# Three loads at the head of the kernel begun by ScalarE's queue in place of SyncE's

## The chip, the cores and the metric

The kernel runs on one core of one Trainium2 chip. The metric is device time in microseconds (us); the time of the kernel before is 755.41 us, the median of 3 runs (755.40 to 755.68). Engines are named as in the profile: PE (TensorE matmul), PEld (its weight loads), DVE (VectorE), ACT (ScalarE), POOL (GpSimd), SP (SyncE). SPq is the instruction queue of SP, from which transfers are begun.

## The reference

An attention with 32 memory slots per head, then two feed-forward layers, in float32:

```
a   = softmax(phi, over the 576 positions)          # (4, 8, 576, 32)
k_m = a^T k ; v_m = a^T v                           # per batch and head: 32 x 64
x   = softmax(q k_m^T / sqrt(64)) v_m               # (4, 8, 576, 64) -> 2304 x 512
h   = x w_in ; g = max(0.01 h, h) ; y = g w_out     # w_in 512x2048, w_out 2048x512
out = ((y w_a) * (y w_b)) w_out2                    # 512x1536, 512x1536, 1536x512
```

## The kernel before

The kernel is one long list of small operations (`op(...)`), each with one engine, what it reads and what it writes. A table written out by hand, ORDER, gives the order in which all of them are emitted, and so the order within each engine's instruction queue; a second table, PLACES, gives each tile its room in SBUF or PSUM (s0 to s36 are rooms of 4 KB per partition). Nothing is reordered afterwards: an engine takes its instructions in the order of the table. Semaphores stand between engines and between a transfer and its users.

Attention goes by batch b (0 to 3) and by group g of four heads (0 and 1). For one (b, g), `kv_part` loads phi and two tiles of k and v (`kv`, 512 KB each, and a rest `kvr`), takes the exponential of phi (L454, ACT, its maximum from DVE at L448), transposes it on PE (`t_a` L503, `t_z` L507/L509) and copies it to SBUF (`en`, L311 on ACT), multiplies it with k and v on PE (`km`, L525), divides by the sum (L541, ACT, `kvn`), transposes the result (`kvt`, L551) and copies it out (`kd` and `vm`, L311). `q_load` brings q; `sc_both` makes the scores (`sc`, L620) and their softmax on DVE and ACT. `vw_unit` multiplies v's part with w_in (L690), `h_unit` makes h (L735).

A weight is loaded by `weight`, in 64-bit words (`raw`, 512 KB, L393), and put into another format by three ACT instructions and two of DVE: high (L403), sign (L410), low (L407), clamp (L414), join (L418). The first two weight tiles of w_in are here called win(0,0) and win(0,1).

Transposes named `warm` fill PE's time at the head; they are counted out in the same table.

All input loads are begun on SP's queue, in the table's order: phi(0,0), phi(0,1), phi(1), win(0,0), kvr, kv(0,1,0), kv(0,1,1), kv(0,0,0), kv(0,0,1), two tiles of q, then win(0,1), win(0,2), win(0,3), two more of q, and so on. Here kv(b, g, i) is the i-th tile of a pair.

What the table has in ACT's order at the head, with the loads of the change at the words where they stand among ACT's instructions:

```
word  6  load phi(0,1)
word  8  exponential of phi(0,0)      word 13  exponential of phi(0,1)
word 20  copy en of group 0           word 24  copy en of group 1
word 26  exponential of phi(1), g=1   word 28  copy en (L516) of t_z of group 0
word 31  load win(0,0)
word 32  high of win(0,0)  (L403)     word 35  copy en (L516) of t_z of group 1
word 37  exponential of phi(1), g=0
word 39  load kv(0,1,0)
word 40  sign of win(0,0)  (L410)
```

PE's order around them: t_z of group 0 (L509), t_z of group 1, transposes of phi(1), km of group 1 from `kvr` (it needs the copy of word 35), four `warm`, a t_z of phi(1), km of group 1 from kv(0,1,0) and kv(0,1,1), km of group 0 in three parts with kvt of group 1 among them, the scores of group 1, kvt of group 0, the scores of group 0.

Rooms: kv(0,1,0) and win(0,1) have the same one (s1), so the load of win(0,1) waits until km of group 1 has read kv(0,1,0). Win(0,2) has the room of win(0,0) (s13) and waits for its low. Win(0,3) has a fresh room and stands behind both on SP's queue.

Of the kernel before, what the change touches and what calls it, by code (L numbers as in the profile page):

```python
# [16 lines left out]
B, H, S, D, M = 4, 8, 576, 64, 32  # L17
DM, DFF, DFF2 = 512, 2048, 1536
P = 128
# [52 lines left out]
def c_dve(n):  # L72
    return 0.16 + n * 1.03e-3
# [6 lines left out]
def c_dma(nbytes):  # L80
    return max(0.6, nbytes / DMA_RATE)
# [195 lines left out]
def tile_mem_attention__leaky_mlp__bilinear_mlp(  # L277
# [13 lines left out]
    nc = tc.nc  # L291
# [8 lines left out]
    op, tile_of = pr.op, pr.tile  # L300
# [80 lines left out]
    def weight(kind, c, k=0, after=(), split=True, late=False):  # L381
        key, raw, low_t = (kind, c, k), ("raw", kind, c, k), ("lw", kind, c, k)
        cv, half = cv_of(kind, c, k)
        tile_of(raw, "slot", [512], I64)
        if cv not in pr.specs:
            tile_of(cv, "slot", [2, 512], I32)
        tile_of(low_t, "t", [512], I32)
        if split:
            tile_of(key, "slot", [2, 512], F32R)

        def load(T):
            src = src_of[kind](c, k)
            nc.sync.dma_start(T[raw] if len(src.shape) == 2 else T[raw].rearrange("p (j f) -> p j f", j=src.shape[1]), src)  # L393

        def words(T, t, w):
            return T[raw].bitcast(t).rearrange("p (n t) -> p n t", t=2)[:, :, w]

        def part(T, t, w):
            return T[low_t].bitcast(t).rearrange("p (n t) -> p n t", t=2)[:, :, w]


        def high(T):
            nc.scalar.activation(T[cv][:, half, :].bitcast(F32), words(T, F32, 1), AF.Abs, scale=2.0 ** 16)  # L403


        def low(T):
            nc.scalar.activation(part(T, U16, 0), words(T, U32, 0), AF.Copy, scale=0.937 * 2.0 ** -29)  # L407

        def sign(T):
            nc.scalar.activation(part(T, F16, 1), words(T, F32, 1), AF.Copy, scale=2.0 ** -120)  # L410

        def clamp(T):
            x = T[cv][:, half, :].bitcast(F32)
            nc.vector.tensor_scalar(x, x, W_LEAST, W_MOST, op0=ALU.max, op1=ALU.min)  # L414

        def join(T):
            x = T[cv][:, half, :]
            nc.vector.scalar_tensor_tensor(x, x, 3, T[low_t], op0=ALU.logical_shift_left, op1=ALU.bitwise_or)  # L418

        a, lt = ("a", key), ("l", key)  # L420
        op("DMA", c_dma(524288), load, r=after, w=[raw], tiles=[raw], ahead=1e12 if late else 45.0)
        op("ACT", 0.66, high, r=[raw], w=[a], tiles=[raw, cv, low_t])
        op("ACT", 0.66, low, r=[raw], w=[lt], tiles=[raw, low_t, cv])
        op("ACT", 0.8, sign, r=[raw], w=[("s", key)], tiles=[raw, low_t, cv])
        op("DVE", 0.42, clamp, w=[a], tiles=[cv])
        op("DVE", 0.68, join, r=[lt, ("s", key)], w=[a], tiles=[cv, low_t])
        if kind == "win" and c == 0 and k > 1:
            idle(cv, lambda t: t[:, half, 0:P].bitcast(F32), a)
        if not split:
            return  # L430
        op(copy_by(512), 0, lambda T, e: copy(e, T[key][:, 0, :], fp(T, kind, c, k)), r=[a], w=[("hi", key)], tiles=[cv, key])
        op("DVE", c_dve(512), lambda T: minus(T[key][:, 1, :], fp(T, kind, c, k), T[key][:, 0, :].bitcast(F32)), r=[a, ("hi", key)], w=[key], tiles=[cv, key])
# [31 lines left out]
    def kv_part(b, g):  # L464

        phi, en, kvn = ("phi", b, g) if b == 0 else ("phi", b), ("en", b, g), ("kvn", b, g)
        kvt = [("kv", b, g, 0), ("kv", b, g, 1)]
        rest = ("kvr", b // 2)

        lot = slice(b % 2 * 64, b % 2 * 64 + 64)  # L470
        if b == 0:
            tile_of(phi, "slot", [1, S])
            op("DMA", c_dma(P * S * 4), lambda T: nc.sync.dma_start(T[phi], phiT[b, :, g:g + 1, :]), w=[("e", b, g)], tiles=[phi])
        elif g == 0:
            tile_of(phi, "big", [2, S])
            op("DMA", c_dma(P * S * 8), lambda T: nc.sync.dma_start(T[phi], phiT[b]), w=[("e", b, 0), ("e", b, 1)], tiles=[phi], keep=2)

        def ph(T):
            return T[phi][:, g if b else 0, :]

        ek = ("e", b, g)
        tile_of(en, "slot", [5, P])
        tile_of(kvn, "t", [2, 2, D])
        for i, k in enumerate(kvt):
            tile_of(k, "slot", [2, 512])
            op("DMA", c_dma(P * 4096), lambda T, i=i, k=k: nc.sync.dma_start(T[k], kv[b, g, :, 2 * i:2 * i + 2, :]), w=[k], tiles=[k], keep=6 if b else 0)
        if g == 0 and b % 2 == 0:
            tile_of(rest, "slot", [2, 512])
            op("DMA", c_dma(P * 4096), lambda T: nc.sync.dma_start(T[rest], kv_rest[b:b + 2].rearrange("b p g f -> (b p) g f")), w=[rest], tiles=[rest], keep=6 if b else 0)

        st = [stat((n, b % 2), 2) for n in ("nmx", "es", "er")]
        er, ker = st[2][:, g:g + 1], ("er", b % 2, g)
        if b == 0:
            phi_stats(b, [g], phi, st)
        elif g == 0:
            phi_stats(b, [0, 1], phi, st)
        ta, tz = ("ta", b, g), ("tz", b, g)
        tile_of(ta, "x", [4, P])
        tile_of(tz, "x", [P])

        def t_a(T):
            for t in range(4):
                nc.tensor.transpose(T[ta][:, t, :], ph(T)[:, t * P:(t + 1) * P], ident)  # L503

        def t_z(T):
            if b % 2:
                nc.tensor.transpose(T[tz], ph(T)[:, S - P:S], ident)  # L507
            else:
                nc.tensor.transpose(T[tz][0:64], ph(T)[:, 4 * P:S], ident)  # L509

        op("PE", 0.45, t_a, r=[ek], w=[ta], tiles=[phi, ta])
        op("PE", 0.12, t_z, r=[ek], w=[tz], tiles=[phi, tz])
        op(copy_by(512), 0, lambda T, e: copy(e, T[en][:, 0:4, :], T[ta]), r=[ta], w=[(en, 0)], tiles=[ta, en])
        if b == 0:
            idle(en, lambda t: t[:, 0, :], (en, 0))
        op(copy_by(128), 0, lambda T, e: copy(e, T[en][lot, 4, :], T[tz][lot]), r=[tz], w=[(en, 1)], tiles=[tz, en])  # L516
        km = ("km", b, g)
        tile_of(km, "x", [P])

        def k_m(T, ts, first, last):  # L520
            for t in ts:
                n = slice(P) if t < 4 else lot
                src = T[kvt[t // 2]][:, t % 2, :] if t < 4 else T[rest][lot, g, :]
                for h in range(4):
                    nc.tensor.matmul(  # L525
                        T[km][h * M:(h + 1) * M, :], T[en][n, t, h * M:(h + 1) * M], src[:, h * P:(h + 1) * P],
                        start=first and t == ts[0], stop=last and t == ts[-1], skip_group_check=True,
                    )

        parts = KM_FIRST[g] if b == 0 else ((0, 1, 2, 3, 4),)  # L530
        for i, ts in enumerate(parts):
            need = list(dict.fromkeys(kvt[t // 2] if t < 4 else rest for t in ts))
            op(
                "PE", 0.29 * len(ts) + 0.05, lambda T, i=i, ts=ts: k_m(T, ts, i == 0, i == len(parts) - 1),
                r=[(en, 0), *([(en, 1)] if 4 in ts else []), *need], w=[km], tiles=[en, *need, km],
            )

        def norm(T, e):
            src = T[km].rearrange("p (c d) -> p c d", c=2).unsqueeze(2).to_broadcast([P, 2, 2, D])
            if e == "ACT":  # L540
                nc.scalar.activation(T[kvn], src, AF.Copy, scale=er)  # L541
            else:
                nc.vector.tensor_scalar_mul(T[kvn], src, er)

        op({"DVE": c_dve(256), "ACT": c_act(256)}, 0, norm, r=[km, ker], w=[kvn], tiles=[km, kvn])
        o = ("kvt", b, g)
        tile_of(o, "x", [2, P])

        def k_t(T):
            for i in range(2):  # L550
                nc.tensor.transpose(T[o][:, i, :], T[kvn][:, i].rearrange("p c d -> p (c d)"), ident)  # L551

        op("PE", 0.25, k_t, r=[kvn], w=[o], tiles=[kvn, o])

        op(copy_by(128), 0, lambda T, e: copy(e, kd[b % 2][:, g, :], T[o][:, 0, :]), r=[o], w=[("kd", b % 2, g)], tiles=[o])
        op(copy_by(128), 0, lambda T, e: copy(e, vm[:, b, g, :], T[o][:, 1, :]), r=[o], w=[("vm", b, g)], tiles=[o])
# [802 lines left out]
    for c, b in UNITS:  # L1359
        p, l = divmod(b, 2)  # L1360
# [20 lines left out]
        else:  # L1381
            if not whole(c, b):
                for j in range(2):
                    g = g_of(c, b, j)
# [85 lines left out]
```

## Time and profile before

| what | value |
|---|---|
| median of 3 runs | 755.41 us |
| the profiled execution | 756.11 us, of which the span is 754.3 us |
| PE busy | 746.6 us (99% of the span) |
| DVE, ACT busy | 688.8 us, 493.3 us |
| chain that ended last | PE 97%, ACT 1%, DMA 1% |
| DMA | 145.75 MB; nearly all engines busy in the first three of 40 slices |

The span is divided in 40 slices on the page; the first is 18.9 us long and holds all that the change touches. An idle time in brackets behind a row is that of the engine just before the instruction, and the arrow names what ended it.

### The profile page before, as it was taken

Reading aid. Unit: us, or ns where it says so; the run is one execution under the profiler, and the core shown is the slowest. Engines: PE = TensorE matmul, PEld = TensorE weight load, DVE = VectorE, ACT = ScalarE, POOL = GpSimd, SP = SyncE. Lnnn points to the kernel's source line nnn. Section 1 sums busy time; section 2 is a strip of 40 time slices with the busy share of each in tenths; the row PEclk is TensorE's granted clock in tenths of the full one; section 3 lists DMA queues with packets and bytes.
Section 4 is the critical chain, followed back from the end, with each engine's and each line's share of the span. In section 5 each row is a group of like instructions: output and inputs, shape, how many; then the busy total and the mean of one; then the engine's idle time right before and its main releaser. Section 6 shows DMA issues by size and latency. Waiting matters only on the chain.

```text
span 754.3 us, 12116 instructions
## 1 busy us (share of the span) xinstructions
PE 746.6 (99%) x4492; PEld 618.5 (82%) x4492; DVE 688.8 (91%) x1115; ACT 493.3 (65%) x962; POOL 3.4 (0%) x9
## 2 busy tenths in 40 slices
PE   8999999999999999999999999999999999999997
PEld 7656788887888789888888888888888888888885
DVE  2899988999999899999988989999999999789897
ACT  5898988796778786965767468487474424534430
POOL 0000000000000000000000000000000000000000
PEclk9999999999999999999999999999999999999999
DMA  9994233531342124167964466588896576584423
GB/s 324 388 407 168 83 113 126 163 117 57 112 139 82 47 84 140 56 209 244 346 219 168 141 207 237 195 280 292 262 382 243 208 259 233 177 309 167 158 72 113
DMA packets 56698, 145.75 MB, mean 193 GB/s; under 512 B 6976, under 2 KB 20544, under 8 KB 56640
## 3 DMA queue, kind: packets, MB, share of 16 engines
q1 hardware_dynamic: 56208, 143.41, 54.0%
q0 software_dynamic: 432, 1.57, 1.1%
q8 instruction: 35, 0.57, 0.3%
q14 instruction: 23, 0.19, 0.1%
HBM read 101.97 MB, written 41.42 MB: 190 GB/s over the span
## 4 chain that ended last, share of the span: by engine, by line
PE 97%; ACT 1%; DMA 1%; DVE 0%; issue 0%; POOL 0%; SPq 0%; POOLq 0%
PE abx L1098 17%; PE h L750 13%; PE ys_x L890 10%; PE abz L1098 9%; PE os_x L1297 8%; PE ys_z L890 5%; PE aby L1098 4%; PE os_z L1297 4%; PE o L1201 4%; PE yl L834 3%; PE ys_y L890 3%; PE a L1143 2%; PE b L1143 2%; PE vw L690 2%; PE os_y L1297 2%; PE y L800 2%
## 5 line engine op out<-in xcount | busy, mean ns | idle before, releaser
L1098 PE MATMUL abx<-yb_T,wo 128*128 128x512 f32 x432 | 108.4, 390 | 0.0
L1098 PEld LDWEIGHTS abx<-yb_T,wo 128*128 128x128 f32 x432 | 80.3, 188 | 16.2
L750 PE MATMUL h<-ahi,vwh 128*128 128x320 f32 (+1 forms) x240 | 73.4, 306 | 0.0
L311 ACT COPY ok<-os_x 128x512 f32<-128x512 f32 x66 | 38.0, 587 | 50.6 <-PE os_x L1297 46.9
L750 PE MATMUL h<-ahi,vwl 128*128 128x320 f32 (+1 forms) x240 | 71.0, 296 | 0.0
L750 PE MATMUL h<-alo,vwh 128*128 128x320 f32 (+1 forms) x240 | 70.9, 296 | 0.0
L711 ACT ACTIVATE bt<-h 128x256 f32<-128x256 f32 x120 | 45.1, 389 | 23.3 <-PE h L750 22.3
L750 PEld LDWEIGHTS h<-ahi,vwh 128*128 128x128 f32 x240 | 45.3, 189 | 12.2 <-issue 3.7
L311 ACT COPY pf<-abx 128x512 f32<-128x512 f32 x48 | 27.8, 585 | 36.7 <-PE abx L1098 35.0
L750 PEld LDWEIGHTS h<-alo,vwh 128*128 128x128 f32 x240 | 45.4, 189 | 1.5
L750 PEld LDWEIGHTS h<-ahi,vwl 128*128 128x128 f32 x240 | 45.4, 189 | 0.0
L316 DVE TENSOR_TENSOR sl_T<-bt,sh_T 128x1024 fp32r<-128x1024 f32 x28 | 34.2, 1221 | 3.0 <-ACT sh_T L311 2.3
L1098 PE MATMUL aby<-yb_B,wo 128*128 128x512 f32 x144 | 36.7, 390 | 0.0
L1098 PE MATMUL abx<-yb_B,wo 128*128 128x512 f32 x144 | 36.7, 390 | 0.0
L1098 PE MATMUL abz<-yb_T,wo 128*128 128x512 f32 x144 | 36.4, 389 | 0.0
L1098 PE MATMUL abz<-yb_B,wo 128*128 128x512 f32 x144 | 36.1, 389 | 0.0
L1297 PE MATMUL os_x<-pb_T,w 128*128 128x512 f32 x132 | 35.2, 389 | 0.0
L316 DVE TENSOR_TENSOR bt<-bt,bt 128x1024 f32<-128x1024 f32 x28 | 34.0, 1220 | 0.8 <-ACT bt L711 0.5
L311 ACT CAST sh_T<-bt 128x1024 fp32r<-128x1024 f32 x26 | 27.3, 1051 | 7.2 <-DVE bt L316 6.9
L311 ACT COPY u<-abx 128x512 f32<-128x512 f32 x24 | 14.0, 586 | 27.6 <-PE abx L1098 26.2
L1098 PEld LDWEIGHTS abz<-yb_T,wo 128*128 128x128 f32 x144 | 27.0, 188 | 5.6
L1098 PEld LDWEIGHTS abz<-yb_B,wo 128*128 128x128 f32 x144 | 26.9, 188 | 5.5
(327 smaller groups left out, 2051.9 us busy)
## 6 DMA issues: line engine op xcount, KB each, us to landing
k_wo<-wo SPq DMA_DIRECT2D x32, 512.0 KB, 5.2
wo<-k_wo SPq DMA_DIRECT2D x32, 512.0 KB, 4.8
raw_wout<-in_w_out_dram SPq DMA_DIRECT2D x24, 512.0 KB, 4.2
raw_win<-in_w_in_dram SPq DMA_DIRECT2D x16, 512.0 KB, 5.5
kv<-in_kv_dram SPq DMA_DIRECT2D x16, 512.0 KB, 9.0
wf<-k_wf SPq DMA_DIRECT2D x11, 512.0 KB, 5.8
raw_wb<-in_w_b_dram SPq DMA_DIRECT2D x8, 512.0 KB, 5.7
raw_wa<-in_w_a_dram SPq DMA_DIRECT2D x8, 512.0 KB, 4.6
```

The costliest lines, as they stand in the source:

```text
L311: nc.scalar.copy(dst, src)
L316: nc.vector.tensor_tensor(dst, a, b, op=alu)
L690: nc.tensor.matmul(rows_of(T, os, b, g, j, i), vm[half, b, g, head], w, start=True, stop=True)
L711: nc.scalar.activation(dst, src, AF.Prelu, alpha=0.01)
L750: nc.tensor.matmul(T[o], T[w[u]][:, k, fs], T[a[v]][:, k, cols], start=k == 0 and y == 0, stop=k == 1 and y == 2)
L800: nc.tensor.matmul(T[o], fp(T, *ws[j])[:, at], T[g_of(c, b, j)][:, i, :], start=f == 0, stop=f == 3)
L834: nc.tensor.matmul(T[o], T[ws[j]][:, u, w_left(c, 2 * eh + j, i, x)], T[hl[v]][:, f, :], start=f == 0 and y == 0, stop=f == 3 and y == 2)
L890: nc.tensor.matmul(T[o], lhs(T, u, w_left(c, 0, kk, x)), T[hl[v]][:, kk, :], start=i in (1, 2, 5) and kk == 0 and y == 0, stop=kk == 1 and ...
L1098: nc.tensor.matmul(T[o], T[w][:, which, u, k * P:(k + 1) * P], T[ys[v]][:, k, :], start=first and k == 0 and x == 0, stop=k == 1 and x == ...
L1143: nc.tensor.matmul(T[o], T[w][:, k // 2, u, k % 2 * P:(k % 2 + 1) * P], T[ys[v]][:, k, :], start=(k == 0 and x == 0), stop=(k == 3 and x = ...
L1201: nc.tensor.matmul(T[o], T[w][:, u, es], right(T, x, v), start=(x == 0 and k == 0), stop=(x == 1 and k == 2))
L1297: nc.tensor.matmul(T[o], lhs(T, u), T[g][:, v, :], start=i in (1, 2, 5) and k == 0, stop=k == 2, skip_group_check=True)
```

## The change

Three of the loads are begun with `nc.scalar.dma_start`, so that the instruction that begins them stands in ACT's queue: phi(0,1), win(0,0) and kv(0,1,0). ORDER and PLACES are the same, so each stands on ACT's queue at the word it has in the table. All other loads stay on SP's queue.

```diff
@@ weight, load
-            nc.sync.dma_start(T[raw] if len(src.shape) == 2 else T[raw].rearrange("p (j f) -> p j f", j=src.shape[1]), src)
+
+            (nc.scalar if key == ("win", 0, 0) else nc.sync).dma_start(T[raw] if len(src.shape) == 2 else T[raw].rearrange("p (j f) -> p j f", j=src.shape[1]), src)
@@ kv_part
-            op("DMA", c_dma(P * S * 4), lambda T: nc.sync.dma_start(T[phi], phiT[b, :, g:g + 1, :]), w=[("e", b, g)], tiles=[phi])
+            op("DMA", c_dma(P * S * 4), lambda T: (nc.scalar if g else nc.sync).dma_start(T[phi], phiT[b, :, g:g + 1, :]), w=[("e", b, g)], tiles=[phi])
@@ kv_part
-            op("DMA", c_dma(P * 4096), lambda T, i=i, k=k: nc.sync.dma_start(T[k], kv[b, g, :, 2 * i:2 * i + 2, :]), w=[k], tiles=[k], keep=6 if b else 0)
+            op("DMA", c_dma(P * 4096), lambda T, i=i, k=k: (nc.scalar if (b, g, i) == (0, 1, 0) else nc.sync).dma_start(T[k], kv[b, g, :, 2 * i:2 * i + 2, :]), w=[k], tiles=[k], keep=6 if b else 0)
```

## Rows read from the trace of the kernel before

**Rows 1.** The page's chain that ended last, share of the span by engine.
```profile
PE 97%; ACT 1%; DMA 1%; DVE 0%; issue 0%; POOL 0%; SPq 0%; POOLq 0%
```
**Rows 2.** Busy time by stretch: PE, PEld, DVE, ACT, POOL, PEclk, DMA share, GB/s.
```profile
24.00:57.00 33.00, 32.47 (x352) 19.12 (x353) 29.59 (x59) 29.20 (x71) 0.00 (x0) 1.00 1.02 399
```
**Rows 3.** Order of time, SP's queue, the first 20 us: start, length, line, transfer.
```profile
0.74 0.87 SPq L473 DMA_DIRECT2D phi<-in_phiT_dram  x2
...
2.12 0.43 SPq L393 DMA_DIRECT2D raw_win<-in_w_in_dram  x1
...
3.11 2.93 SPq L486 DMA_DIRECT2D kv<-in_kv_dram  x4
6.08 1.62 SPq L568 DMA_DIRECT2D q<-in_qT_dram  x2
13.39 1.42 SPq L393 DMA_DIRECT2D raw_win<-in_w_in_dram  x3
```
**Rows 4.** Waits of SP's queue from 7.7 to 14 us: total, times, longest.
```profile
SPq L393 <- DMA kv<-in_kv_dram: 3.7, 1, 3.7
SPq L393 <- PE km L525: 1.9, 1, 1.9
```
**Rows 5.** Order of time, ACT, the first 20 us.
```profile
3.84 1.28 ACT L454 ACT_TABLE_LOAD   x1 [3.84 <-DMA phi<-in_phiT_dram]
...
10.16 0.25 ACT L311 COPY en<-tz 64x128 f32<-64x128 f32 x1
10.30 0.69 ACT L403 ACTIVATE cv_win<-raw_win 128x512 f32<-128x512 f32 x1
...
11.82 0.77 ACT L410 ACTIVATE lw_win<-raw_win 128x512 f16<-128x512 f32 x1
...
16.30 0.47 ACT L541 ACTIVATE kvn<-km,er 128x256 f32<-128x256 f32 x1
18.72 0.27 ACT L311 COPY kd<-kvt 128x128 f32<-128x128 f32 x1 [1.95 <-PE kvt L551]
...
19.66 0.68 ACT L403 ACTIVATE cv_win<-raw_win 128x512 f32<-128x512 f32 x1 [0.50 <-DMA raw_win<-in_w_in_dram]
```
**Rows 6.** Order of time, PE, 9 to 20 us.
```profile
9.14 0.27 PE L509 MATMUL tz<-ident,phi 128*64 128x128 f32 x1
...
11.64 0.42 PE L525 MATMUL km<-kvr,en 64*32 64x128 f32 x8
...
12.69 1.08 PE L525 MATMUL km<-kv,en 128*32 128x128 f32 x32
...
15.59 0.64 PE L525 MATMUL km<-kv,en 128*32 128x128 f32 x16
17.68 0.64 PE L620 MATMUL sc<-q,kd 64*32 64x256 f32 x8 [1.45 <-DMA q<-in_qT_dram]
18.25 0.44 PE L551 MATMUL kvt<-ident,kvn 128*128 128x128 f32 x2
```
**Rows 7.** Issues of 512 KB loads: the last figure is us to landing.
```profile
raw_wout<-in_w_out_dram SPq DMA_DIRECT2D x24, 512.0 KB, 4.2
...
raw_wa_-1_3787<-in_w_a_dram SPq DMA_DIRECT2D x1, 512.0 KB, 3.4
```
**Rows 8.** The loads of raw_win issued in the first 40 us.
```profile
DMA to landing us min/median/max: 6.2/7.1/10.4
```
**Rows 9.** Busy time by stretch, columns as in Rows 2: a short gap, and the end.
```profile
16.00:17.00 1.00, 0.23 (x10) 0.00 (x0) 0.23 (x2) 0.74 (x2) 0.00 (x0) 1.00 1.05 385
...
751.00:752.50 1.50, 0.11 (x2) 0.00 (x0) 0.36 (x1) 0.00 (x0) 0.00 (x0) 1.00 0.85 305
...
753.50:754.30 0.80, 0.00 (x0) 0.00 (x0) 0.00 (x0) 0.00 (x0) 0.00 (x0) 0.50 0.00 0
```
**Rows 10.** Pieces of the chain that ended last: start, length, what.
```profile
1.36 6.20 PE warm L343 x36
...
8.00 0.44 PE warm L343 x4
```

## The prediction

> **What bounds the kernel now.** I read the page's chain of waits first: 97% of it is PE [rows 1], so what counts is how late PE's steady work begins and whether anything holds it up afterwards. The busy time by stretch shows where it becomes steady: from 24 to 57 us PE is busy 32.47 of 33 us [rows 2], and from there to the end I found no stall that could take a delay back. In that stretch the DMA share is 1.02 as well, so the transfers have no room to catch up either. A delay D at about 24 us is therefore D at the end, and the question is D. For it I read the first 20 us in order of time, queue by queue: SP, ACT, PE [rows 3 to 6]. What the reader is to see there is that SP's queue begins win(0,0) at 2.12 and the four kv tiles from 3.11 on, long before anyone needs them, because SP has nothing else to do. ACT comes to the same words of the table much later: the copy in front of win(0,0) runs at 10.16 and the sign behind kv(0,1,0) at 11.82 [rows 5].
>
> **phi(0,1).** It is the first instruction of ACT's queue, so nothing holds it; it leaves at about 0.74 beside phi(0,0) in place of 0.43 later (two issues take 0.87 [rows 3]). Gain: at most that 0.43. Loss: phi(0,0) now shares the DMA engines and may land later by about the same, and it releases ACT's first work at 3.84. PE has its 36 counted `warm` to 7.56 [rows 10], which cover half a microsecond either way. I take 0, ends -0.4 and +0.4.
>
> **win(0,0).** The load now stands behind the copy of word 28. Does ACT's queue hold it there? The trace has no load begun by ACT; the nearest rows say yes. ACT's table load reads no data of this program and still began at 3.84, when phi had landed [rows 5]: it stood behind a wait. And on SP's queue the three loads of raw_win leave together at 13.39 [rows 3], although the third has a free room: it stood behind the first. So the load leaves when the copy's own wait is over, which is t_z's end on PE at 9.14 + 0.27 = 9.41 [rows 6], or at the latest when the engine has done the copy, 10.41 [rows 5]. I take 9.45: instructions start before the one ahead has ended (10.30 against 10.16 + 0.25 [rows 5]), so the queue is ahead of the arithmetic. To landing: 3.4 us is a quiet load of the same size, 4.2 the median of 24 [rows 7], and 6.2 the fastest raw_win of the head, where all loads stood in one row [rows 8]. ACT's load has a row of its own, but shares the engines with SP's kv tiles; I take 4.2, so T = 13.7, ends 12.8 and 16.6. Its high, with the rest of ACT's queue behind it, begins at 13.7, not 10.30. That alone would cost little; kv behind it is worse.
>
> **kv(0,1,0).** Ahead of it on ACT's queue stand the high, which waits for T, a copy and an exponential. It leaves between T (the queue ahead of the arithmetic) and T + 1.52 (from 10.30 to 11.82 [rows 5]); I take 14.0, near the first for the reason above. By then SP's first loads are nearly through, so the landing is the quiet one: 14.0 + 3.4 = 17.4, ends 16.2 (12.8 + 3.4) and 22.3 (16.6 + 1.52 + 4.2). Before, it had landed at 11.4: SP's two q loads end at 7.70 [rows 3], and SP then waited 3.7 us for it [rows 4]. PE's km of group 1 began at 12.69 [rows 6]; now it begins at 17.4, later by 4.7.
>
> **What that becomes.** From the start of this km to the end of the last km of group 0 PE needed 16.23 - 12.69 = 3.54 us [rows 6], then it waited 1.45 for q. That q lands no later now, since the same bytes are asked for and two loads have gone to the back. So the scores begin at 20.9, not 17.68, and the 1.45 is slack. Group 0 follows: kvn 0.07 after its km and 0.47 long, kvt 0.44, the copies [rows 5, 6]. After them ACT was idle for 0.50 until win(0,1) landed [rows 5]. SP may begin win(0,1) only when km has read kv(0,1,0), because they share a room (the 1.9 us wait [rows 4]); it left 0.70 after km's start and now leaves at 18.1, with a quiet queue ahead: 21.5 to 22.3 by 3.4 and 4.2. ACT is ready for it at 22.4, so the 0.50 is slack too. D1 = 4.7 - 1.45 - 0.50 = 2.75. The queue of the transfers stands nearly empty from about 17 to 20; everything behind win(0,1) on SP moves by about 2 to 3 us, no more than the engines do, so it adds nothing.
>
> **The clock.** PE's fillers are counted out, so the new waits leave it idle: from about 11.6, until ACT's copy releases the km from `kvr` [rows 6] at about 14.6, and again until 17.4, with about 1.3 us of work between. [...] Its price is in the first row of the chain: the 36 `warm` took 6.20 us from a cold start, at 0.11 each they would have taken 3.96 [rows 10], a loss of 2.24. Of the 4.6 us from km at 17.4 to kvt at 22.0, 0.54 is ACT, so 88% of it bears: D2 = 2.0, ends 0 and 2 x 2.24.
>
> **Sum.** The profiled execution is 756.11 us, 754.3 of it span; 756.11 + 2.75 + 2.0 = 760.9. It lies 0.70 above the median, so the median goes from 755.41 to 760.2.
>
> **Rivals.**
> *The clock holds* (0.22): gaps of 3 and 2 us with some work between are not the empty end of the kernel. Then D = 2.75: 758.2, own range 757.0 to 760.
>
> *ACT's queue runs ahead of waits* (0.20), the case in which it is not slower. The place is the hand-over to ACT: if an instruction that waits is set aside and the queue goes on, the loads leave while the earlier instructions still wait. It decides at two points: win(0,0) must leave by about 6.1 (10.30 - 4.2) and kv(0,1,0) by about 8.5 (12.69 - 4.2). Then nobody waits for either, the same bytes pass through full engines, and only the 0.43 of the first issue is left: 755.0 to 755.6, nearest 755.2. Against it speak the table load behind phi and the third raw_win behind the first [rows 3, 5]; for it, that neither row is a load on ACT. [...] No run before shows a load on ACT, and the row on the table load disagrees with an open-ended queue.
>
> *Two rows of transfers are faster than one* (0.04): the engines would have to bring the head's bytes 1.5 us sooner. The DMA share there is at 1.0 in nearly all of it, as it is later [rows 2], which leaves it little: 753.5.
>
> *The landings are at their late ends* (0.04): T = 16.6 and kv(0,1,0) near 20: 763.
>
> **How the numbers follow.** The forecast itself has 0.50, with its own range 758.5 to 762.5 (T from 12.8 to 15, D2 from 1.2 to 3). Under 0.2%, 1.5 us, a measurement of this kernel can't tell a change from none, so faster ends at 753.9 and slower begins at 756.9. Slower: 0.50 + 0.04 + nearly all of 0.22, about 0.75. Same: 0.20 and a little of the clock's rival, 0.21. Faster: 0.04. The range from 755.0 to 762.5 leaves out the fast case, the lower edge of the queue's rival and the late landings, some 0.15.
>
> **What would show it.** Right: ACT's row for the high of win(0,0) at about 13.7 with its idle time ended by raw_win's DMA; PE's km from kv at about 17.4, its idle time ended by kv's DMA; SP's raw_win at about 18 in place of 13.39; the 1.45 wait for q gone; a granted clock below 1.00 near 16 to 22; PE's later rows all moved by one amount. Wrong: loads on ACT's queue leaving before 6 and 8.5; the km from kv near 12.7; or steady PE work beginning later than before and the end not.

## The result: 0.94% slower, and the profile after

The changed kernel takes 762.69 us (median of 4 runs, 762.55 to 762.81) against 755.45 for the kernel before on the same chip: a ratio of 1.0094, interval 1.0082 to 1.0106, or 7.24 us more. Its profiled execution is 762.55 us with a span of 760.8; that of before was 756.11 with 754.3. In the traces the move is 6.44.

Line numbers are one higher than before from L394 on. First the page's shares of the chain that ended last, then pieces of it in order of time (start, length, what). They answer to [rows 1, 10].

```profile
PE 98%; DMA 1%; DVE 0%; issue 0%; POOL 0%; ACT 0%; POOLq 0%
```

```profile
1.36 6.72 PE warm L343 x36
...
9.90 0.07 ACT phi L455
9.97 5.26 DMA raw_win<-in_w_in_dram
15.27 3.70 DMA kv<-in_kv_dram
19.01 2.52 PE km L526 x40
```

Two transfers stand one behind the other in the middle of the head, and PE's km follows them. The chain before had ACT's work there, and then the transfer of win(0,1):

```profile
14.35 5.84 DMA raw_win<-in_w_in_dram
```

ACT in order of time (the bracket is the idle time before a row, and what ended it) shows why; it answers to [rows 5], and SP's queue after it to [rows 3]:

```profile
0.74 0.41 ACTq L474 DMA_DIRECT2D phi<-in_phiT_dram  x1
4.12 1.28 ACT L455 ACT_TABLE_LOAD   x1 [4.12 <-DMA phi<-in_phiT_dram]
...
9.90 0.78 ACT L455 ACTIVATE phi<-phi,nmx 128x576 f32<-128x576 f32 x1
9.97 0.39 ACTq L394 DMA_DIRECT2D raw_win<-in_w_in_dram  x1
...
10.68 0.25 ACT L311 COPY en<-tz 64x128 f32<-64x128 f32 x1
15.25 0.66 ACT L404 ACTIVATE cv_win<-raw_win 128x512 f32<-128x512 f32 x1 [4.33 <-DMA raw_win<-in_w_in_dram]
15.27 0.35 ACTq L487 DMA_DIRECT2D kv<-in_kv_dram  x1
15.82 0.24 ACT L311 COPY en<-tz 64x128 f32<-64x128 f32 x1
...
26.00 0.69 ACT L404 ACTIVATE cv_win<-raw_win 128x512 f32<-128x512 f32 x1
```

```profile
3.76 1.83 SPq L569 DMA_DIRECT2D q<-in_qT_dram  x2
20.15 1.42 SPq L394 DMA_DIRECT2D raw_win<-in_w_in_dram  x3
```

Win(0,0) left at 9.97, though nothing kept its room: it stood behind the copy of word 28, which waits for t_z. Kv(0,1,0) left at 15.27, the moment the high of win(0,0) could start. On PE the same rows are (answering to [rows 6]):

```profile
9.66 0.27 PE L510 MATMUL tz<-ident,phi 128*64 128x128 f32 x1
...
16.11 0.42 PE L526 MATMUL km<-kvr,en 64*32 64x128 f32 x8 [3.89 <-ACT en L311]
...
19.01 1.93 PE L526 MATMUL km<-kv,en 128*32 128x128 f32 x32 [1.59 <-DMA kv<-in_kv_dram]
...
23.97 0.64 PE L526 MATMUL km<-kv,en 128*32 128x128 f32 x16
24.54 0.64 PE L621 MATMUL sc<-q,kd 64*32 64x256 f32 x8
...
31.61 1.99 PE L736 MATMUL h<-at,vwf 128*128 128x256 f32 x8
```

The km from kv starts 6.32 later than at 12.69, takes 1.93 instead of 1.08, and the 1.45 wait for q is gone. The first h was at 25.24 before and is 6.37 later. Busy time by stretch (columns as in Rows 2; the seventh figure, ahead of the DMA share, is the granted clock) shows the gap, the fall, and then the steady stretch:

```profile
12.00:13.00 1.00, 0.22 (x3) 0.00 (x0) 0.00 (x0) 0.00 (x0) 0.00 (x0) 1.00 1.09 389
13.00:14.00 1.00, 0.00 (x0) 0.00 (x0) 0.00 (x0) 0.00 (x0) 0.00 (x0) 1.00 1.01 371
14.00:15.00 1.00, 0.00 (x0) 0.00 (x0) 0.00 (x0) 0.00 (x0) 0.00 (x0) 1.00 0.32 119
15.00:16.00 1.00, 0.00 (x0) 0.00 (x0) 0.05 (x1) 0.75 (x3) 0.00 (x0) 1.00 0.00 0
16.00:17.00 1.00, 0.89 (x12) 0.69 (x13) 0.37 (x1) 1.00 (x4) 0.00 (x0) 0.95 0.46 115
17.00:18.00 1.00, 0.42 (x3) 0.03 (x1) 0.00 (x0) 1.00 (x3) 0.00 (x0) 0.50 0.95 332
...
20.00:21.00 1.00, 1.00 (x24) 0.58 (x20) 0.00 (x0) 0.00 (x0) 0.00 (x0) 0.50 0.00 0
...
60.00:749.00 689.00, 688.13 (x3901) 577.72 (x3898) 644.59 (x1027) 453.27 (x871) 2.71 (x3) 1.00 0.52 180
```

The last row holds 688.13 us of PE work in 689; the same stretch before, 6.4 us earlier (53.6 to 742.6), held the same 688.13. Nothing behind the head changed; it only starts later.

### The profile page after: what moved, and what is told of

Its sections match the earlier page's. It is cut to its first block, busy times and chain, and to the rows that moved or that the text cites. A ratio compares the mean times of both kernels' runs of the same rounds, so it can differ in the third digit from the quotient of the medians.

```text
span 760.8 us, 12116 instructions
## 1 busy us (share of the span) xinstructions
PE 749.8 (99%) x4492; PEld 620.3 (82%) x4492; DVE 688.6 (91%) x1115; ACT 493.7 (65%) x962; POOL 3.4 (0%) x9
## 3 DMA queue, kind: packets, MB, share of 16 engines
q10 hardware_dynamic: 560, 1.34, 0.5%
## 4 chain that ended last, share of the span: by engine, by line
PE 98%; DMA 1%; DVE 0%; issue 0%; POOL 0%; ACT 0%; POOLq 0%
PE abx L1099 17%; PE h L751 13%; PE ys_x L891 10%; PE abz L1099 9%; PE os_x L1298 8%; PE ys_z L891 5%; PE aby L1099 4%; PE os_z L1298 4%; PE o L1202 4%; PE yl L835 3%; PE ys_y L891 3%; PE vw L691 2%; PE a L1144 2%; PE b L1144 2%; PE os_y L1298 2%; PE y L801 2%
```

## Experiments

The reason of the prediction: a load begun on ACT's queue waits for ACT's earlier instructions, so two loads land late; PE waits, and its granted clock falls. The rivals: the second queue as such costs time, ACT's queue runs ahead of its waits, or the clock plays no part. A further question came with the 5.26 us of win(0,0). Does a later load share the DMA engines evenly with SP's, or is it served after all that was begun before it?

**One load of the three at a time.**

```diff
 e1: only phi(0,1) on nc.scalar; win(0,0) and kv(0,1,0) on nc.sync
 e2: only win(0,0) on nc.scalar
 e3: only kv(0,1,0) on nc.scalar
```

> Only phi(0,1) is begun by ACT; win(0,0) and kv(0,1,0) are back on SP. Queue-order theory (a load on ACT leaves when the waits ahead of it on ACT's queue are over): it is first there, so no change: 755.4, between 755.0 and 756.0. Rival (ACT's row of transfers is slow in itself, wherever the load stands): phi(0,1) lands late and ACT's exponentials with it; still covered by PE's fillers up to some 1 us, then 756 to 757.

Measured: 755.20, ratio 0.9993 (0.9984 to 1.0002; the ratios of the experiments are to runs of the kernel before made beside them, 755.67 to 755.83). The step on phi(0,1) costs nothing.

> Only win(0,0) is begun by ACT. Queue order: it leaves near 10, as in the changed kernel. If transfers are served in the order in which they were begun, whichever queue began them, it lands after all of SP's, which now hold 512 KB more: near 16.4, km from kv starts 2.2 later at 18.6, and with a fallen clock the time is about 761.4. If the two rows share the engines evenly, it lands near 13.8, km from kv starts near 16, and the time is 757 to 759. If the delay of the changed kernel is kv(0,1,0)'s alone, 755.4.

Measured: 761.69, ratio 1.0078 (1.0064 to 1.0092). The chain and ACT's row:

```profile
9.54 6.90 DMA raw_win<-in_w_in_dram
```

```profile
16.47 0.66 ACT L404 ACTIVATE cv_win<-raw_win 128x512 f32<-128x512 f32 x1 [5.92 <-DMA raw_win<-in_w_in_dram]
```

Kv(0,1,0) was back on SP and in time, and still 6.0 of the 7.2 us were lost. The copy that km needs stands behind the high on ACT, so win(0,0) alone holds PE. Its 6.90 to landing is what service in the order begun gives, with one kv tile more ahead of it: it landed at 16.44, and 16.4 was expected. It left at 9.54, 0.87 after t_z's end (8.40 + 0.27) but with the exponential of word 26 (9.53), whose wait for its maximum ended last of those ahead.

> Only kv(0,1,0) is begun by ACT; win(0,0) comes early from SP, so ACT's high does not wait. Queue order: the load leaves when the copy of word 35 may go, near 10.9. Served in the order begun: it lands after SP's last, near 16.5, later than needed by 3.8; 1.95 of that is slack, and the clock may fall: 757.3 to 759.3. Shared evenly: it lands near 14.2 and slack covers it: 755.4 to 755.8.

Measured: 760.98, ratio 1.0066 (1.0052 to 1.008), a miss: kv was expected at 16.5 and the time at 757.3 to 759.3.

```profile
10.48 7.56 DMA kv<-in_kv_dram
```

```profile
18.08 1.94 PE L526 MATMUL km<-kv,en 128*32 128x128 f32 x32 [5.72 <-DMA kv<-in_kv_dram]
```

From 15 to 18 us the DMA share was only 0.55, 0.12 and 0.06 (206, 37 and 24 GB/s) while this load was still under way. Why its last part was so slow, the runs do not show. The two loads are not additive: either alone costs 5.3 to 6.0 us, both together 7.2.

**The queue without the waits.** The loads are moved in ORDER to the front of ACT's queue.

```diff
-14 7 13 17 6 10 38 21 22 ... 15 8 241 242 ... 62 20 39 244
+14 7 13 17 6 10 38 241 39 21 22 ... 15 8 242 ... 62 20 244
```

> The changed kernel with the words of the loads win(0,0) and kv(0,1,0) moved in the table to the front of ACT's queue, right behind phi(0,1): all three are begun by ACT before its first wait. Queue order: no wait of the changed kernel is left, 755.0 to 755.9, the same as before within 0.2%. Rival (ACT's row itself is slow or served last, wherever its loads stand): kv(0,1,0) lands after SP's last, 15 or later, and the time is 757 to 759.

Measured: 755.73 (11 runs), ratio 1.0001 (0.9992 to 1.001). The loads leave at 0.74, 1.17 and 1.66, km starts at 13.03, and the clock stays at 1.00. The same three loads on the same second queue cost nothing, so the loss is their place behind ACT's waits.

**The clock.** 34 identity transposes after a `ta` and 13 after a `tz` of (1,1) keep PE busy in the gaps of the changed kernel.

```diff
 # both for (b, g) == (1, 1)
+for _ in range(34): nc.tensor.transpose(T["warm",], ident, ident)   # after t_a
+for _ in range(13): nc.tensor.transpose(T["warm",], ident, ident)   # after t_z
```

> The changed kernel with 47 more fillers on PE: 34 transposes of the identity behind the transposes of phi(1), 13 behind the t_z after them, 0.11 us each, so that PE works through the two gaps. The loads stand where they stood. If the fallen clock is a part of the loss, its 2.06 us come back and the granted clock stays at 1.00: 760.4 to 761.0. If the clock costs nothing because PE only waits there, 762.7.

Measured: 760.94, ratio 1.0068 (1.0054 to 1.0082), as expected: 1.75 less than the changed kernel, or 2.13 less when each is held against the kernel before of its own runs. The clock was 1.00 all through, on PE:

```profile
19.49 1.08 PE L530 MATMUL km<-kv,en 128*32 128x128 f32 x32 [0.43 <-DMA kv<-in_kv_dram]
...
30.20 0.88 PE L625 MATMUL sc<-q,kd 64*32 64x320 f32 x16 [1.12 <-DMA q<-in_qT_dram]
```

From this km to the end of the last km of group 0 PE took 3.53 us here and 5.60 in the changed kernel (23.97 + 0.64 - 19.01). The last row above is a new wait: with PE faster, the second pieces of q, which SP begins behind win(0,3), came 1.12 too late and took back half of it in this execution. At 761.84 it is the longest of the four, 0.90 above their median; whether the others have that wait is not shown.

**Earlier on ACT, but behind SP's bytes.** ORDER has the two loads (241 and 39, taken from their old places) behind ACT's second exponential, where they leave before anyone needs them.

```diff
-... 12 3 58 41 42 5 2 24 ...
+... 12 3 58 41 42 241 39 5 2 24 ...
```

> The words of the loads win(0,0) and kv(0,1,0) moved to stand behind the second exponential on ACT's queue. Queue order: they leave when that exponential's wait is over, near 5.2 and 5.7, though the engine is still loading its table then. Served in the order begun: they land behind SP's kv tiles, win(0,0) near 12.5 and kv(0,1,0) near 14.5, km from kv is 1.5 to 2 late, which the slack of 1.95 covers: 755.4 to 756.5. Shared evenly: 755.4. If ACT's loads left only when the engine had done what stands ahead, near 6.8: 756 to 758.

Measured: 759.39, ratio 1.0047 (1.0033 to 1.0061), a miss of 3 us. The chain, then ACT:

```profile
5.58 8.67 DMA raw_win<-in_w_in_dram
```

```profile
14.27 0.66 ACT L404 ACTIVATE cv_win<-raw_win 128x512 f32<-128x512 f32 x1 [4.61 <-DMA raw_win<-in_w_in_dram]
```

Win(0,0) left 4.39 us earlier than in the changed kernel and landed only 0.98 earlier (14.25 against 15.23). The expectation had it behind SP's kv tiles alone, near 12.5. The first load of q, begun at 4.12, stood ahead of it as well; the second, begun at 5.63, came after it (5.58).

**More bytes ahead, and fewer.** In e8 win(0,1) and win(0,2) get rooms of their own, so that SP begins its three raw_win loads ahead of ACT's win(0,0). In e12 the two q loads of 256 KB go behind win(0,1).

```diff
 e8, PLACES:  raw win(0,1) s1 -> s34, raw win(0,2) s13 -> s29
 e12, ORDER:
-... 56 36 30 53 54v 31 247 55a 87 ...
+... 30 53 54v 31 247 56 36 55a 87 ...
```

> The changed kernel with win(0,1) and win(0,2) given rooms of their own, so that SP begins them, and win(0,3), near 6 us and waits for nobody. Served in the order begun: 1.5 MB more stands ahead of ACT's win(0,0), which lands near 19, kv(0,1,0) near 22.5, and the time is about 766. Shared evenly: win(0,0) lands near 14 to 15 as before and the time stays at 762 to 763. If SP's wait for the room carries the delay of the changed kernel: 757 to 760.

> The changed kernel with SP's two q loads moved behind its load of win(0,1): about 0.5 MB fewer are begun ahead of win(0,0), which still leaves near 9.9. If the 5.26 us of win(0,0) in the changed kernel was the loads begun ahead of it (theory: served in the order begun), it lands 3.4 to 4.2 us after it left, so the high begins at 13.3 to 14.1, kv(0,1,0) leaves there and PE's km from kv begins at 17.0 to 17.7, the value of the forecast (17.4) and not 19.0. If the long landing belongs to ACT's queue whatever is ahead, it stays at 5 to 5.5 and km at 18.7 to 19.2. The time itself is then set by q, which leaves only near 18 and is awaited until about 22.5: 761 to 763.5.

E8: 769.61, ratio 1.0181 (1.0165 to 1.0196), beyond even the order-begun theory's figure: kv(0,1,0), begun at 18.78, took 6.97 in its turn, with three more loads of q and kv begun by SP in between (12.77 to 14.13). Its chain:

```profile
2.59 8.73 DMA kv<-in_kv_dram
...
11.35 7.39 DMA raw_win<-in_w_in_dram
18.78 6.97 DMA kv<-in_kv_dram
```

Win(0,0) left 1.43 after t_z's end (9.65 + 0.27): the chain has it follow the landing, at 11.32, of a kv load that SP began at 2.59.

E12: 762.65, ratio 1.0098 (1.0082 to 1.0114). Its chain and PE:

```profile
9.34 4.60 DMA raw_win<-in_w_in_dram
13.97 4.07 DMA kv<-in_kv_dram
```

```profile
18.08 1.93 PE L526 MATMUL km<-kv,en 128*32 128x128 f32 x32 [1.94 <-DMA kv<-in_kv_dram]
```

In duration the 4.60 lies between the two theories of its expectation (up to 4.2, or from 5), and so does km at 18.08 (up to 17.7, or from 18.7). The first h, at 30.98, is only 0.63 sooner than in the changed kernel, because the scores now wait 0.46 for q; the four runs spread from 761.83 to 765.37. In time of landing the kernels line up:

| kernel | begun ahead, against the changed kernel | left | landed |
|---|---|---|---|
| e12 | 0.5 MB less (two q) | 9.34 | 13.94 |
| changed | | 9.97 | 15.23 |
| e2 | 0.5 MB more (kv(0,1,0) on SP) | 9.54 | 16.44 |
| e8 | 1.8 MB more (three raw_win, one q) | 11.35 | 18.74 |
| e7 | 0.25 MB less (the second q) | 5.58 | 14.25 |

In e12 and e2, 0.5 MB less or more begun ahead moves the landing by 1.2 to 1.3 us; 512 KB take 1.34 at the 390 GB/s that the changed kernel's transfers reach from 28 to 60 us. In e8 it is 3.5 us for the 1.8 MB, of which about 0.2 were still to move when win(0,0) landed. When the load left hardly counts: e7's left 4.39 us earlier and landed 0.98 earlier.

The packets of the two queues show it directly. In the changed kernel SP's queue moved 0.76 MB from 10 to 12 us and ACT's not one packet, though win(0,0) had left at 9.97; between its start and its landing SP's queue moved 1.13 MB, the rest of what it had begun. Nor does SP's queue always go first: in e8, when win(0,0) landed, SP's queue had moved 5.2 MB, less than the 5.4 MB begun before it, and the loads that SP began after it followed. For a load that comes to a backlog this is service nearly in the order begun, across both queues, and not even sharing from its start. In e3 the landing came later than this.

It does not hold at the front. In e4 both queues have loads from 1.2 us on, and they move side by side: from 5 to 9 us 0.73 MB on ACT's queue and 0.93 MB on SP's. Win(0,0), begun at 1.17 with phi(0,0) and phi(0,1) (0.6 MB) ahead of it, landed only at 8.7, when SP's queue had moved 1.6 MB. What decides between the two ways, the runs do not show.

**A version that beats both, and what makes it so.** E9 is e4's order with e8's rooms. E10 is the kernel before with the rooms alone, all on SP. E11 is e9's order and rooms with all loads on SP.

```diff
 e9:  after.  ORDER as in e4, PLACES as in e8
 e10: before. PLACES as in e8
 e11: before. ORDER as in e4, PLACES as in e8
```

> Both at once: the three loads at the front of ACT's queue, and rooms of their own for win(0,1) and win(0,2). Nothing waits for a room or stands behind a wait, the engines of the transfers have no hole near 14 to 16, win(0,1) lands near 16.5 in place of 18.4. If the head is held by that landing: 753.5 to 754.5, faster than both kernels. If it is held by q, the scores and the softmax: 755 to 755.7.

Measured: 754.44 (11 runs), ratio 0.9981 (0.9972 to 0.999): 0.19% faster than before. Km starts at 12.16, and win(0,1) lands at 18.02.

> The kernel before, all loads on SP, its order of the table, with the two new rooms alone (win(0,1) in s34, win(0,2) in s29). SP's three loads of raw_win should leave near 7.7 instead of 13.39, and the high of win(0,1) begin near 18.1 without its wait of 0.50; PE's km from kv stays near 12.7 and the scores' wait for q stays. Theory A (what the kernel with the front order and the rooms gained is the rooms' doing): 754.3 to 755.0. Theory B (the gain needs the loads on ACT's queue): 755.3 to 756.0.

Measured: 755.54 (11 runs), ratio 0.9996 (0.9988 to 1.0005): the rooms alone bring nothing, so theory A falls.

> The same table and rooms as the kernel that was a little faster than both (three loads at the front, two new rooms), with all loads on SP's queue. Theory A (order of the loads and rooms, not the queue): 754.1 to 754.9, PE's km from kv near 12.3, the 1.45 wait for q gone or under 0.5. Theory B (the second queue brings it): 755.2 to 755.9.

Measured: 758.15 (6 runs, 756.85 to 760.70), ratio 1.0038 (1.0024 to 1.0051), slower than either theory had it. The trace is that of the fastest run, so it accounts for some 1.1 of the 2.4 us. On one queue the two moved loads stand ahead of phi(1). DVE's row:

```profile
10.83 1.35 DVE L448 TENSOR_REDUCE nmx<-phi 128x2 f32<-128x1152 f32 x1 [4.53 <-DMA phi<-in_phiT_dram]
```

Phi(1) lands so late that ACT and PE wait for its exponential, and km starts at 15.06. On two queues, in e4 and e9, SP begins phi(1) at about 1.2, beside ACT's win(0,0) and not after it. So the second queue can help when its loads stand at the front: 754.44 with it and the rooms, 755.54 with the rooms alone.

## Where the prediction held, and the step that failed

The direction, the chain of waits and the fall of the clock were right; the time was not. It lies at 762.69, above the end of the range at 762.5: 4.75 us of move were expected and 7.24 measured. Of the 2.49 between them, 1.06 are the landing of win(0,0), 0.52 its start, 0.11 kv and the clock, and 0.80 the level.

- **phi(0,1)**: 0 expected. The table load behind phi(0,0) begins at 4.12, not 3.84, inside the 0.4 allowed, and e1 measures nothing.
- **ACT's queue holds the loads**: right. Win(0,0) left 0.04 after t_z's end (9.66 + 0.27), as taken. The 0.52 by which that is later than 9.45 is the 36 `warm` (6.72 instead of 6.20; 5.46 to 7.08 in the kernels tried). The rival of 755.2 had the queue go on past an instruction that waits; the rows at 9.97 and 15.27 disagree with it.
- **The failed step, win(0,0) to landing**: 4.2 taken, 5.26 measured. The prediction held that a row of its own would let ACT's load share the engines with SP's kv tiles, and its range took the landing T to be 15 at most. The table of landings and the packets show that it is served after nearly all of them, q included: T was 15.23. Kv's own landing was 3.70 for 3.4, but it left with the high, 0.25 sooner than taken. Together: 0.52 + 1.06 - 0.25 + 0.30 = 1.6 us, which is km at 19.01 instead of 17.4. The rival of late landings (763, given 0.04) came nearest in time, but its T of 16.6 and kv near 20 were not reached: its time is met because of the level, below.
- **Slack**: both pieces were used up, as taken. The wait for q is gone, and the high at 26.00 waits for no transfer.
- **Clock**: 5.60 - 3.54 = 2.06 for a forecast of 2.0. No run shows the 2.0 as it was worked out: its price was read from the 36 `warm` as a cold start, and the trace of the kernel before has the granted clock at 1.00 over them (2 to 6 us), so that the size fits is in part luck. What the runs showed in its place: in the changed kernel the granted clock was 0.50 from 17 to 23 us and this stretch took 2.06 longer, and in e6, at 1.00, it took 3.53 instead of 5.60. The rival in which the clock holds is out.
- **The sum of the traces**: 6.32 + 2.06 - 1.95 = 6.43, and the trace moved by 6.44.
- **The level**: the medians moved 0.8 more than the traces. The prediction took 1.95 of slack from an execution that was 0.70 above its kernel's median, and then took the 0.70 off again. If that execution was long because of its wait for q, an ordinary one has less slack to give, and the loss is larger by as much. For this speaks that e1 and e10 have no wait for q in their traces, with spans 0.9 and 1.1 shorter. In e1's trace, an execution at its kernel's median, the first h begins at 24.35, 7.26 before the 31.61 of the changed kernel. It is not shown: other executions of the kernel before left no trace.

## What to carry to other kernels

A load belongs on an engine's queue only where no waiting instruction stands ahead of it. A second queue whose loads stood at the front cost nothing here, while the same loads in the middle of ACT's work cost 7 us, because a chain of transfers formed that SP had hidden. To say when a load lands that comes to a backlog, add its own bytes to those begun before it and not yet moved, on all queues, and divide by the rate. It is a rough rule: at 390 GB/s it gives 3.2, 4.3, 6.3, 7.8 and 6.8 us for win(0,0) in e12, the changed kernel, e2, e8 and e7, which took 4.60, 5.26, 6.90, 7.39 and 8.67. And look whether a slack is there in an ordinary execution before it is set against a loss.

## What the runs showed of the hardware

- A load that came to a backlog was served nearly in the order begun, whichever queue began it: win(0,0) took 4.60, 5.26, 6.90, 7.39 and 8.67 us to landing in five kernels, by the bytes ahead of it. Where both queues began their loads in the first 2 us (e4), they moved side by side, 0.73 and 0.93 MB from 5 to 9 us.
- The last packets can be slow: in the changed kernel the engines' share was 0.32 from 14 to 15 us and 0.00 from 15, and win(0,0) landed at 15.23. In e3 the load was under way until 18 us, at a share of 0.06 to 0.12 from 16 us on.
- ACT begins a transfer as soon as the waits ahead are over, and before the arithmetic ahead has ended: at 9.97 beside an exponential of 9.90 to 10.68, and at 15.27 beside a high that began at 15.25, with a copy and an exponential still to come in between. In e8 it also waited for the landing of an earlier load (11.32).
- One stall of PE was charged twice: the wait, and 2.06 us in the work behind it, at a granted clock of 0.50 from 17 to 23 us.
